# Batch 0 of a convolution and low-rank mixer kernel: U in float32 on a hardware queue, x in pieces of 8, 6 and 3 tiles, and h of group 0 from four partial sums

## The chip, the cores and the metric

The kernel runs on one core of a Trainium2 chip. The metric is the device time of one execution in microseconds (us). A core has a matrix engine (TensorE, "PE", with its weight loads listed apart as "PEld"), VectorE (DVE), ScalarE (ACT), GpSimd (POOL) and SyncE (SP). PE writes its results to PSUM, which has eight banks here; ACT and DVE copy them out to SBUF ("evacuate" them). Data come from the chip's main memory by 16 DMA engines. POOL's loads go through a software queue and can change the type on the way (float32 to bfloat16); loads issued by SP and ACT go through hardware queues.

## The reference

```python
# x: (8, 4224, 192), weight: (8 heads, 7 taps), U: (4224, 32), V: (32, 4224)
w = exp(weight - weight.max(-1, keepdims=True)); w = w / (w.sum(-1, keepdims=True) + 1e-9)
x_pad = concat([zeros((B, 6, D)), x], axis=1)              # causal, along the sequence
y[b, s, h*24 + g] = sum_k w[h, k] * x_pad[b, s + k, h*24 + g]
hT = y.transpose(0, 2, 1) @ U @ V                          # mixes along the sequence
u  = y + hT.transpose(0, 2, 1)
out = u + maximum(u @ w_ch1, 0) @ w_ch2                    # 192 -> 768 -> 192
```

Each head's convolution has 7 taps that are the softmax of its row of `weight`. All inputs and the output are float32; the kernel computes in bfloat16 with float32 sums.

## The kernel before, in words

**Tiles and groups.** The sequence of each of the 8 batches is cut into 33 tiles of 128 positions. `y[b]` holds a batch as 128 positions x 33 tiles x 192 channels. Eight consecutive tiles, counted over all batches, form a group; there are 33 groups. For each group the kernel makes `u`, transposes it to channels on partitions (`uT`), multiplies by W1 with a relu (`w1`, PE line 590, evacuations at lines 601 and 603), multiplies by W2 and adds `u` (`w2`, line 614), and stores (line 629).

**Batch 0, the part before group 0.** This is a chain of its own, in the order in which the code is written (the order of each engine's instructions is the order of the code; nothing is rearranged):

- `w_sb` comes by SP's queue (L61). x of batch 0 lies in SBUF as 64-row blocks, two halves of partitions (`r` = 0 and 1), and is loaded by POOL in two pieces, of 13 and 4 tiles per half (`KP`, L86 to L95, L135; issued at L79).
- POOL makes index patterns with iota (`dif`, `tap`, `fp`, `efp`, L101 to L123). DVE compares them to one-hot patterns, takes the softmax (L192 to L213, the exponential on ACT at L201), and forms `pr` (L223). `band_half` sums `pr` with seven products by the identity (L231) and copies the result to `band`, the banded matrix of a head's taps, by four evacuations on ACT (L240) for each half of the heads.
- POOL loads U as bfloat16 (`Ur`, L130 and L134), V's first 2,048 columns (`V0_sb`, 32 partitions, L139), W1 in four loads (L143), V (L153, L160), W2 (L164), then x of batch 1.
- `idle` runs matrix products of zeros (L173), 60 ahead of the band and 30 ahead of the convolution, each of 128 columns.
- `conv` (L368) makes y by products of `band` with x (L381), with one evacuation by ACT and one by DVE (`evac`, L272 and L274) for each call. Piece 0 has one call for each of the 8 heads, piece 1 two calls of 4 heads.
- `u_layout` (L276) rearranges U by products with `Eq` (L281) into `U_sb`, with tiles' positions on partitions.
- `yT_part(0)` (L542) starts `uT` of group 0 in three banks with products by the identity (L548).
- `tt` is yT U for the batch, 32 ranks x 192 channels. `tt_mm` (L405) lets four tiles work at once, so that it leaves four partial sums in four groups of 32 partitions. For batch 0 the first piece's partial sums go to `tf` (`tt_first`), a product by `R4f` (L701) adds them and repeats the sum on all four groups, and `tt_more` (L451) adds the tiles of the second piece with weights repeated four times (`U4_sb`, L435). `tt_done` copies the result out (L461).
- `hT_part(0)` (L558) adds V0 times tt to the three banks (L563), and ACT and DVE copy them out as `uT`. Then `w1(0)` starts. After it, `hT_part(1)` does the same for group 1.

**Later batches.** `tt_split` copies the partial sums as a bfloat16 value and a bfloat16 remainder (`hi`, `lo`, L425), `tt_sum` adds the four groups by `R4` (L467), and the work is placed between the groups by the hand-written table `SLOTS`. Loads of later batches are held until a named product of `w1` has ended (`held`, `LOADS`), and from batch 2 on POOL makes a shifted copy of x (`x_shift`, L306 to L318) for a convolution in 32-column tiles (`conv32`, L352).

Of the kernel before, what the change touches and what calls it, by code (L numbers as in the profile page):

```python
# [7 lines left out]
ALU = mybir.AluOpType  # L8
# [6 lines left out]
def kernel(  # L15
# [43 lines left out]

    w_sb = cst.tile([P, H, KC], F32, name="w_sb")  # L60
    nc.sync.dma_start(out=w_sb[:], in_=weight[:].partition_broadcast(P))  # L61
    xt = [None] * B
# [23 lines left out]
    KP = [(0, 13), (13, NB1 // 2)]  # L86

    def x_piece(k):
        for r in range(2):
            k0, k1 = KP[k]  # L90
            k1 = min(k1, (NB0, NB1)[r] // 2)
            x_part(0, r, (1 - r if k == 0 else 2 * k0 + 1), 2 * k1 + 1)

    x_tile(0)
    x_piece(0)  # L95
# [5 lines left out]
    dif = cst.tile([P, BW], F32, name="dif")  # L101
    for r in range(4):
        nc.gpsimd.iota(
            dif[QB * r : QB * r + QB, :],
            pattern=[[1, BW]],
            base=0,
            channel_multiplier=-1,
            allow_small_or_imprecise_dtypes=True,
        )
    tap = cst.tile([P, KC], F32, name="tap")  # L110
    nc.gpsimd.iota(
        tap[:],
        pattern=[[-1, KC]],
        base=HW,
        channel_multiplier=0,
        allow_small_or_imprecise_dtypes=True,
    )

    fp = cst.tile([P, P], I32, name="fp")
    nc.gpsimd.iota(fp[:], pattern=[[1, P]], base=P, channel_multiplier=-1)  # L120

    efp = cst.tile([P, 4, P], I32, name="efp")
    nc.gpsimd.iota(efp[:], pattern=[[-1, 4], [1, P]], base=4 * P, channel_multiplier=-4)  # L123


    NUB = (NT + 3) // 4
    Ur = cst.tile([P, NUB, 4 * R], BF16, name="Ur")
    U4 = moe_U[:].rearrange("(n a) r -> n (a r)", a=4)
    nfull = NT // 4
    nc.gpsimd.dma_start(  # L130
        out=Ur[:, 0:nfull, :], in_=U4[0 : nfull * P, :].rearrange("(k p) c -> p k c", p=P)
    )
    nlast = NT * 32 - nfull * P
    nc.gpsimd.dma_start(out=Ur[0:nlast, nfull, :], in_=U4[nfull * P :, :])  # L134
    x_piece(1)  # L135


    V0_sb = cst.tile([32, 2 * GT * P], BF16, name="V0_sb")
    nc.gpsimd.dma_start(out=V0_sb[:], in_=moe_V[:, 0 : 2 * GT * P])  # L139
# [27 lines left out]
    zz = cst.tile([P, 512], BF16, name="zz")  # L167
    nc.vector.memzero(zz[:])  # L168

    def idle(n, w):  # L170
# [6 lines left out]
    idle(60, P)  # L177
# [5 lines left out]
    x_zero(0, nc.vector)  # L183
    hot = cst.tile([P, KC, BW], BF16, name="hot")
# [4 lines left out]
        op=ALU.is_equal,  # L189
    )  # L190
# [10 lines left out]
    nc.scalar.activation(e_sb[:], d_sb[:], ACT.Exp)  # L201
    ident = cst.tile([P, P], BF16, name="ident")
# [18 lines left out]
    def band_half(hh):  # L221
# [16 lines left out]
        for r in range(4):  # L238
            o = QB * (r % 2)
            nc.scalar.activation(  # L240
                out=band[QB * r : QB * r + QB, HQ * hh : HQ * hh + HQ, o : o + BW],
                in_=bp[QB * r : QB * r + QB, 0 : HQ * BW].rearrange("p (h t) -> p h t", h=HQ),
                func=ACT.Copy,
            )

    band_half(0)
    band_half(1)


    Eq = cst.tile([P, 4, P], BF16, name="Eq")  # L250
    nc.vector.tensor_scalar(
        out=efp[:], in0=efp[:], scalar1=P - 1, scalar2=None, op0=ALU.bitwise_and
    )
    nc.vector.tensor_scalar(
        out=Eq[:], in0=efp[:], scalar1=0.0, scalar2=None, op0=ALU.is_equal
    )
    nc.vector.tensor_scalar(
        out=fp[:], in0=fp[:], scalar1=R - 1, scalar2=None, op0=ALU.bitwise_and
    )
    R4f = cst.tile([P, P], F32, name="R4f")  # L260
    nc.vector.tensor_scalar(
        out=R4f[:], in0=fp[:], scalar1=0.0, scalar2=None, op0=ALU.is_equal
    )
    R4 = cst.tile([P, P], BF16, name="R4")
    nc.vector.tensor_copy(out=R4[:], in_=R4f[:])

# [9 lines left out]
    def u_layout():  # L276
# [12 lines left out]
        for jj in range(4):  # L289
            evac(  # L290
                "AD"[jj % 2],
                U_sb[:, 0 : nb[jj], jj, :],
                up[jj][:, 0 : nb[jj] * R].rearrange("p (k r) -> p k r", r=R),
            )

# [72 lines left out]
    def conv(b, h0, nh, rs, engs, k0=0, k1=NT):  # L368
# [4 lines left out]
        pp = {r: bank() for r in rs}  # L373
# [31 lines left out]
    def tt_mm(b, js, p=None, o=0):  # L405
# [3 lines left out]
        for n, j in enumerate(js):  # L409
            c = n % 4  # L410
            nc.tensor.matmul(  # L411
                out=p[32 * c : 32 * c + 32, o : o + D],
                lhsT=U_sb[:, j // 4, j % 4, :],
                rhs=yt[b][:, j, :],
                start=(n < 4),
                stop=(n + 4 >= len(js)),
# [11 lines left out]

    def tt_first(p, js, rest):


        U4_sb = cst.tile([P, sum(b - a for a, b in rest), 4, R], BF16, name="U4_sb")
        n = 0
        for a, b in rest:
            nc.vector.tensor_copy(  # L435
                out=U4_sb[:, n : n + b - a, :, :],
                in_=U_sb[:]
                .rearrange("p k j r -> p (k j) r")[:, a:b, :]
                .unsqueeze(2)
                .to_broadcast([P, b - a, 4, R]),  # L440
            )
            n += b - a
        p = tt_mm(0, js, p, 256)
        t = sml.tile([P, D], F32, name="tt_f", bufs=1)
        evac("A", t[:], p[:, 256 : 256 + D])
        return U4_sb, t

# [241 lines left out]
    for h in range(H):  # L689
        conv(0, h, 1, [0, 1], "AD", *KP[0])  # L690
# [108 lines left out]
```

## Time and profile before

| | us |
|---|---|
| median of 9 runs (lowest to highest) | 330.86 (330.03 to 331.65) |
| the profiled execution's own time | 330.86 |
| its span | 328.9 |
| PE busy | 318.9 (97%) |
| DVE busy | 268.7 (82%) |
| ACT busy | 171.0 (52%) |
| POOL busy | 141.9 (43%) |
| x_sb, first load of batch 0: issue to landing | 7.2 |
| x_sb, second load of batch 0: issue to landing | 10.1 |
| Ur, first load: issue to landing | 8.3 |
| V0 (V_sb, 128 KB): issue to landing | 8.1 |

Times in the profile are counted from the start of the span. A line such as `12.98 2.44 DVE y_sb L274 x6` in the chain of waits is start, length, engine, tile, line of the code and number of instructions; each piece of the chain is what released the next. In the timeline a line is start, length, engine, line, operation, what is written from what, shapes, count, and in brackets how long the engine was idle before and what it waited for. A busy PE is not a PE at its peak, because products overlap. KB of a load are counted as written.

### The profile page before, as it was taken

How to read it: one execution, taken by the hardware profiler on the slowest of the kernel's cores; microseconds unless marked ns; L12 is line 12 of the kernel's file. 1: busy time of each engine (PE TensorE's matmuls, PEld its weight loads, DVE VectorE, ACT ScalarE, POOL GpSimd, SP SyncE). 2: the span in 40 equal slices, each digit the busy share in tenths (PEclk: the TensorE clock that was granted, in tenths of full speed). 3: DMA queues.
4: the chain of work that ended last, by engine and by line, in shares of the span. 5: the costliest groups of instructions: out<-in, count | busy, mean ns of one | idle time of the engine just before them, and what ended most of it. 6: DMA issues, size and time to landing. Idle time of an engine off the chain costs nothing.

```text
span 328.9 us, 9736 instructions
## 1 busy us (share of the span) xinstructions
PE 318.9 (97%) x4072; PEld 224.4 (68%) x4072; DVE 268.7 (82%) x547; ACT 171.0 (52%) x351; POOL 141.9 (43%) x109
## 2 busy tenths in 40 slices
PE   7889999999999999999999999999999999999995
PEld 7655676567647846966874785587797487487495
DVE  5757999996986997798698789879897897896863
ACT  1658444563586098158519807843902912912910
POOL 8580229854995695968659599000000000000000
PEclk9999999999999999999999999999999999999999
DMA  8999996799999899699889969039559159249035
GB/s 102 192 171 165 155 204 153 145 191 158 264 200 171 163 185 199 158 225 200 171 201 169 202 162 216 24 100 240 74 135 261 39 132 216 88 117 268 3 121 169
DMA packets 122908, 53.54 MB, mean 163 GB/s; under 512 B 87760, under 2 KB 122832, under 8 KB 122864
## 3 DMA queue, kind: packets, MB, share of 16 engines
q1 hardware_dynamic: 84672, 38.18, 50.7%
q0 software_dynamic: 38192, 14.73, 38.9%
q8 instruction: 32, 0.52, 0.7%
q14 instruction: 12, 0.10, 0.1%
HBM read 29.49 MB, written 25.95 MB: 169 GB/s over the span
## 4 chain that ended last, share of the span: by engine, by line
PE 78%; POOL 8%; DMA 7%; DVE 3%; ACT 3%; issue 1%; POOLq 0%; DVEq 0%
PE ps L614 37%; PE ps L590 32%; DMA x_sb<-in_x_dram 7%; POOL xb_sb L318 5%; PE ps L352 3%; PE ps L496 3%; ACT rl_sb L601 2%; PE ps L411 2%; DVE y_sb L274 2%; POOL x_sb L79 1%; POOL xb_sb L306 1%; DVE rl_sb L603 1%; PE ps L381 0%; PE ps L467 0%; DVE uT L274 0%
## 5 line engine op out<-in xcount | busy, mean ns | idle before, releaser
L601 ACT ACTIVATE rl_sb<-ps 128x512 bf16<-128x512 f32 x235 | 125.3, 605 | 111.0 <-PE ps L590 99.1
L614 PE MATMUL ps<-W_sb,rl_sb 128*128 128x192 bf16 x1584 | 141.7, 246 | 0.2
L614 PEld LDWEIGHTS <-rl_sb 128*128 128x128 bf16 x1584 | 128.0, 98 | 13.4 <-issue 12.8
L590 PE MATMUL ps<-uT,W_sb 64*128 64x512 bf16 x1188 | 132.0, 376 | 0.8 <-DVE uT L274 0.8
L603 DVE TENSOR_SCALAR rl_sb<-ps 128x512 bf16<-128x512 f32 x161 | 104.3, 689 | 17.7 <-PE ps L590 17.4
L590 PEld LDWEIGHTS <-W_sb 64*128 64x128 bf16 x1188 | 63.9, 94 | 64.6 <-issue 5.0
L622 DVE TENSOR_TENSOR out_sb<-ps,u_sb 128x384 f32<-128x384 f32 (+1 forms) x133 | 70.3, 550 | 24.8 <-PE ps L614 22.4
L318 POOL COPY xb_sb<-x_sb 32x3072 bf16<-32x3072 bf16 (+1 forms) x24 | 67.6, 2824 | 0.7
L518 DVE TENSOR_TENSOR u_sb<-y_sb,ps 128x192 bf16<-128x192 bf16 (+1 forms) x168 | 66.3, 461 | 0.0
L306 POOL COPY xb_sb<-x_sb 128x3072 bf16<-128x3072 bf16 x12 | 32.7, 2742 | 29.7 <-PE ps L352 15.9
L272 ACT ACTIVATE y_sb<-ps 128x384 bf16<-128x384 f32 (+3 forms) x90 | 36.9, 504 | 10.4 <-PE ps L352 7.6
L79 POOL DMA_DIRECT2D x_sb<-in_x_dram x32 | 27.0, 851 | 27.2 <-PE ps L590 16.2
L274 DVE CAST y_sb<-ps 128x408 bf16<-128x408 f32 (+2 forms) x42 | 20.8, 549 | 3.6 <-PE ps L381 2.9
L496 PE MATMUL ps<-tt_sb,V_sb 32*128 32x192 bf16 x264 | 12.6, 246 | 0.8 <-DVE tt_sb L461 0.6
L352 PE MATMUL ps<-xb_sb,band 64*32 64x384 bf16 (+1 forms) x192 | 12.4, 332 | 0.5 <-POOL xb_sb L318 0.5
L352 PE MATMUL ps<-x_sb,band 64*32 64x384 bf16 x192 | 12.1, 333 | 0.0
L496 PEld LDWEIGHTS <-V_sb 32*128 32x128 bf16 x264 | 4.7, 92 | 8.2 <-issue 8.2
L173 PE MATMUL ps<-zz 128*128 128x128 bf16 x90 | 7.9, 271 | 1.2 <-DVE zz L168 1.2
L173 PEld LDWEIGHTS <-zz 128*128 128x128 bf16 x90 | 7.6, 128 | 1.2 <-DVE zz L168 1.2
L352 PEld LDWEIGHTS <-band 64*32 64x32 bf16 x384 | 4.6, 89 | 4.8 <-issue 3.7
L381 PE MATMUL ps<-x_sb,band 64*64 64x312 bf16 (+3 forms) x192 | 7.2, 277 | 0.7 <-DMA x_sb<-in_x_dram 0.7
L425 ACT ACTIVATE tt_hi<-ps 128x192 bf16<-128x192 f32 x7 | 2.3, 331 | 10.8 <-PE ps L411 10.8
(64 smaller groups left out, 71.8 us busy)
## 6 DMA issues: line engine op xcount, KB each, us to landing
out_dram<-out_sb SPq DMA_DIRECT2D x131, 192.0 KB, 2.9
x_sb<-in_x_dram POOLq DMA_DIRECT2D x14, 384.0 KB, 7.3
x_sb<-in_x_dram POOLq DMA_DIRECT2D x7, 432.0 KB, 7.3
x_sb<-in_x_dram POOLq DMA_DIRECT2D x7, 408.0 KB, 6.7
x_sb<-in_x_dram POOLq DMA_DIRECT2D x1, 648.0 KB, 10.1
x_sb<-in_x_dram POOLq DMA_DIRECT2D x1, 624.0 KB, 7.2
uT<-u_sb SPq DMA_TRANSPOSE x31, 4.4
W_sb<-in_moe_w_ch_dram POOLq DMA_DIRECT2D x2, 192.0 KB, 5.3
```

The costliest lines, as they stand in the source:

```text
L79: return nc.gpsimd.dma_start(out=xt[b][HB * r : HB * r + HB, s0:s1, :], in_=x[b, blk * HB : (blk + s1 - s0) * HB, :].rearrange("(j p) d -> ...
L272: nc.scalar.activation(out=out, in_=in_, func=ACT.Copy)
L274: nc.vector.tensor_copy(out=out, in_=in_)
L306: nc.gpsimd.tensor_copy(out=xbt[b][:, s0:s1, :], in_=xt[b][:, s0 + 1 : s1 + 1, :])
L318: nc.gpsimd.tensor_copy(out=xbt[b][q, s0:s1, :], in_=xt[b][q, s0:s1, :])
L352: nc.tensor.matmul(out=pp[r][QB * cg : QB * cg + QB, 0 : nk[r] * GS], lhsT=w[hr], rhs=t[hr, st : st + 2 * nk[r] - 1 : 2, hs], start=True, ...
L518: nc.vector.tensor_tensor(out=u_group(g)[:, i : i + n, :, hf, :], in0=yt[b][:, run[0] : run[0] + n, :].rearrange("p n (c k) -> p n c k", c=3),
L590: last = nc.tensor.matmul(out=pp[hf][:], lhsT=W1_sb[HB * hf : HB * hf + HB, c, m * P : (m + 1) * P], rhs=uTt[g][HB * hf : HB * hf + HB, :, ...
L601: nc.scalar.activation(out=rl[:, m, hf, :], in_=pp[hf][:], func=ACT.Relu)
L603: nc.vector.tensor_scalar_max(out=rl[:, m, hf, :], in0=pp[hf][:], scalar1=0.0)
L614: nc.tensor.matmul(out=cps[:, a * D : (a + 1) * D], lhsT=rlt[g][:, m, hf, (i + a) * P : (i + a + 1) * P], rhs=W2_sb[:, m, :], start=(m == ...
L622: nc.vector.tensor_tensor(out=o[:, 0:n, :].rearrange("p n (c k) -> p n c k", c=3), in0=cps[:, 0 : n * D].rearrange("p (n c k) -> p n c k", ...
```

## The change

- U is loaded as float32 by two loads on ACT's hardware queue, issued ahead of x. ACT copies it to bfloat16 after the exponential. `u_layout` moves ahead of `band_half`; all four of its evacuations are on ACT.
- x of batch 0 comes in pieces of 8, 6 and 3 tiles (2 in the first half). The two halves of a piece are loaded by calls of their own; the first half of piece 0 goes ahead of the iotas, the second half after three of them.
- `dif` is one iota and gets its offsets by a DVE addition of `rq`; `efp` is float32 and is compared with `rq`, so the bit operations on it go. The second half of `band` is evacuated by ACT and DVE in turn.
- `V0_sb` has 128 partitions: V's first 1,024 columns stand on all four groups of 32, by four loads.
- Fillers: 140 of 16 columns and 20 of 128 ahead of `u_layout`, 20 of 64 and 20 of 32 around the second half of `band`.
- Piece 0 of conv takes two heads a call, piece 1 three, three and two, piece 2 four and four; pieces 1 and 2 share two pairs of banks.
- `tt` of batch 0 stays four partial sums in one bank. `tt_split` makes hi and lo of all 128 rows, and `hT_part(0)` multiplies both with the 128-row `V0_sb`, which adds the groups in the product. `tt_first`, `tt_more`, `R4f` and `U4_sb` go. For group 1, `tt_sum(0)` runs after `w1(0)`.

```diff
@@ ahead of x
+    Uf = cst.tile([P, NUB, 4 * R], F32, name="Uf")
+    nc.scalar.dma_start(
+        out=Uf[:, 0:nfull, :], in_=U4[0 : nfull * P, :].rearrange("(k p) c -> p k c", p=P)
+    )
+    nc.scalar.dma_start(out=Uf[0:nlast, nfull, :], in_=U4[nfull * P :, :])
@@ POOL's order
-    KP = [(0, 13), (13, NB1 // 2)]
+    KP = [(0, 8), (8, 14), (14, NB1 // 2)]
-    x_piece(0)
+    x_piece(0, 0)
-    for r in range(4):
-        nc.gpsimd.iota(dif[QB * r : QB * r + QB, :], ...)
+    iota(dif[:], [[1, BW]], 0, -1)
+    iota(tap[:], [[-1, KC]], HW, 0)
+    iota(efp[:], [[-1, 4], [1, P]], 0, -4)
+    x_piece(0, 1)
     nc.gpsimd.iota(fp[:], pattern=[[1, P]], base=P, channel_multiplier=-1)
-    nc.gpsimd.dma_start(out=Ur[:, 0:nfull, :], ...)
-    nc.gpsimd.dma_start(out=Ur[0:nlast, nfull, :], in_=U4[nfull * P :, :])
-    x_piece(1)
-    V0_sb = cst.tile([32, 2 * GT * P], BF16, name="V0_sb")
-    nc.gpsimd.dma_start(out=V0_sb[:], in_=moe_V[:, 0 : 2 * GT * P])
+    for k in (1, 2):
+        for r in range(2):
+            x_piece(k, r)
+    V0_sb = cst.tile([P, 2 * GT * P], BF16, name="V0_sb")
+    for r in range(4):
+        w = (2 if r == 0 else 1) * GT * P
+        nc.gpsimd.dma_start(out=V0_sb[QB * r : QB * r + QB, 0:w], in_=moe_V[:, 0:w])
@@ fillers, patterns, band
+    rq = cst.tile([P, 2], F32, name="rq")
+    for r in range(4):
+        for n, v in enumerate((32.0, -128.0)):
+            nc.vector.memset(rq[QB * r : QB * r + QB, n : n + 1], v * r)
-    idle(60, P)
+    idle(140, 16)
+    idle(20, P)
+    nc.vector.tensor_scalar(
+        out=dif[:], in0=dif[:], scalar1=rq[:, 0:1], scalar2=None, op0=ALU.add
+    )
...
+    nc.vector.tensor_scalar(
+        out=Eq[:], in0=efp[:], scalar1=rq[:, 1:2], scalar2=None, op0=ALU.is_equal
+    )
     nc.scalar.activation(e_sb[:], d_sb[:], ACT.Exp)
+    nc.scalar.activation(out=Ur[:, 0:nfull, :], in_=Uf[:, 0:nfull, :], func=ACT.Copy)
+    nc.scalar.activation(out=Ur[0:nlast, nfull, :], in_=Uf[0:nlast, nfull, :], func=ACT.Copy)
...
-    band_half(0)
-    band_half(1)
+    u_layout()
+    band_half(0, "A")
+    idle(20, 64)
+    band_half(1, "AD")
+    idle(20, 32)
@@ h of a group
     def hT_part(g, tp, engs):
+        ts = ttb[0] if g == 0 else [ttb[0]]
+        k = P if g == 0 else R
+        for n, t in enumerate(ts):
+            for c in range(3):
+                for hf in range(2):
+                    nc.tensor.matmul(
+                        out=tp[c][HB * hf : HB * hf + HB, :],
+                        lhsT=t[0:k, HB * c : HB * c + HB],
+                        rhs=V0_sb[0:k, (2 * g + hf) * 4 * P : (2 * g + hf + 1) * 4 * P],
+                        start=False, stop=(n + 1 == len(ts)), tile_position=(0, HB * hf),
+                    )
@@ the chain before group 0
-    idle(30, P)
-    for h in range(H):
-        conv(0, h, 1, [0, 1], "AD", *KP[0])
-    u_layout()
+    for h in range(0, H, 2):
+        conv(0, h, 2, [0, 1], "AD", *KP[0])
     yT = yT_part(0)
-    U4_sb, tf = tt_first(ps0, ...)
-    for h in range(0, H, 4):
-        conv(0, h, 4, [0, 1], "AD", *KP[1])
-    nc.tensor.matmul(out=ps0[:, 0:D], lhsT=R4f[:], rhs=tf[:], start=True, stop=False)
-    tt_more(ps0, U4_sb, rest)
-    tt_done(0, ps0)
+    ps0 = tt_mm(0, js[0], last=False)
+    work = [{0: bank(), 1: bank()} for _ in range(2)]
+    for n, (h, nh) in enumerate(((0, 3), (3, 3), (6, 2))):
+        conv(0, h, nh, [0, 1], "AD", *KP[1], pp=work[n % 2])
+    for n, h in enumerate(range(0, H, 4)):
+        conv(0, h, 4, [0, 1], "AD", *KP[2], pp=work[1 - n % 2])
+    tt_mm(0, js[1], ps0, first=False, last=False)
+    tt_mm(0, js[2], ps0, first=False)
+    tt_split(0, ps0)
     hT_part(0, yT, "AD")
@@ after w1(0)
+                tt_sum(0)
                 hT_part(1, yT_part(1), "AD")
```

## The prediction

> **What bounds the kernel now.** I read the chain of waits first, cut to the first 45 us, since every edit but one lies ahead of the first matmul of group 0 (L590). Columns: start, length, what.
>
> ```profile
> 1.26 1.12 POOL x_sb L79
> 2.38 10.07 DMA x_sb<-in_x_dram
> ...
> 12.49 0.47 PE ps L381 x6
> 12.95 0.02 issue
> 12.98 2.44 DVE y_sb L274 x6
> ...
> 19.77 0.37 DVE tt_sb L461
> 20.14 0.04 issue
> 20.18 0.42 PE ps L563 x2
> ...
> 21.52 1.08 PE ps L590 x6
> 22.61 4.50 ACT rl_sb L601 x9
> 27.11 0.29 ACT uT L272
> ```
>
> The first 12.45 us are the landing of the second half of piece 0; then 9.03 us of work, mostly evacuations, bring the first L590 at 21.52. After that ACT paces group 0. Later the chain is mostly PE; where it passes to POOL, POOL's load at 61.62 waited 1.39 us for an L590 matmul. So time won ahead of 21.52 should reach the end nearly whole.
>
> Next the stretches of 1 us (busy time of PE, PEld, DVE, ACT, POOL, then clock, DMA share, GB/s), and the timeline of POOL and ACT:
>
> ```profile
> 2.00:3.00 1.00, 1.00 (x13) 1.00 (x11) 0.00 (x0) 0.03 (x1) 1.00 (x2) 1.00 0.09 22
> 3.00:4.00 1.00, 1.00 (x12) 1.00 (x11) 0.00 (x0) 0.00 (x0) 0.82 (x4) 1.00 0.75 61
> 4.00:5.00 1.00, 1.00 (x12) 1.00 (x10) 0.39 (x2) 0.00 (x0) 0.88 (x5) 1.00 1.29 146
> 5.00:6.00 1.00, 1.00 (x13) 1.00 (x11) 0.75 (x6) 0.25 (x1) 1.00 (x2) 1.00 1.60 190
> ```
> ```profile
> 8.69 2.44 ACT L240 ACTIVATE band<-ps 32x152 bf16<-32x152 f32 x8 [2.99 <-PE ps L231]
> ...
> 12.73 0.63 POOL L143 DMA_DIRECT2D W_sb<-in_moe_w_ch_dram  x1 [2.93 <-DMA x_sb<-in_x_dram]
> ...
> 18.57 3.38 POOL L79 DMA_DIRECT2D x_sb<-in_x_dram  x4
> ```
>
> The DMA engines fill only from 5 us on; until about 19 us they then hold some 190 GB/s. `band` was ready at 11.13, so x came last. The tenth POOL load, a piece of W1, waited for the second to land: the trace looks like eight loads open at a time.
>
> **U ahead of x.** Two POOL issues (0.92 and 0.53 us) go; two issues on ACT's queue come, each like w_sb's on SP (0.40), ahead of a table load of 1.28, with ACT idle until 5.45. U is 540 kB read either way. An x packet writes 384 B for 768 B read, and 495 of them in the full us at 5 read 380 kB; U is thus 1.4 us of the engines. Between 2 and 5 us they moved 341 kB less than 3 x 190, that is 1.8 us lie free. So U costs x between 0 and 1.4 us; I take 0.7, as its landing reaches into the full time.
>
> When does U land? The hardware queue's nearest rows are w_sb (128 packets, 2.9 us) and a store of out (256 packets, 2.0 us from issue to landing in the quiet stretch 319.7 to 321.4). w_sb, issued at 0.75, had 7 packets out before 2.0, so some 1.1 us pass first; a store then has 0.9 for 256, 3.5 ns each. U has 1,024 and 32: 0.75 + 1.1 + 3.5, I take **5.3**. The high end is w_sb's pace, 107 packets in the us from 2 to 3, near 10 ns: 10.3 us, a landing at 12. The low end, twice the stores' pace, is 3.7. The wait for U is new: ACT's copies stand before it, and behind them on ACT the evacuations of U_sb and of both halves of band, for which all of conv waits.
>
> The Trainium skill, "DMA: Bandwidth & Descriptors", section "Issuing engines are not separate DMA queues", speaks against this edit: loads of all queues share the same 16 engines, so another queue saves issue time only. By the rule alone x pays the full 1.4 us and conv starts 0.7 later than my sum; the trace's free 1.8 us is why I charge half.
>
> **Piece 0 of 8 tiles.** 384 + 408 KB are 811 kB against 1,303. By the 1-us rows 811 kB of x have gone by 8.2 us and 1,303 by 10.8; the old piece landed at 12.45, 1.65 behind the mean, which I scale to 1.0. Landing: 8.2 + 1.0 + 0.7 = **9.9** (9.2 to 10.6). Pieces 1 and 2 (576 and 240 KB, 3.1 and 1.3 us) land near 14.0 and 15.5; old piece 1, behind the same U and x, landed at 15.99.
>
> **The band.** dif's iota was four (0.84), now one (0.2), but fp's now stands behind the issue of x's second half (0.9) and DVE's ident waits for it, with the softmax queued behind. POOL: 1.26 + 0.84 issue, iotas to 3.2, issue to 4.1, fp to 4.35. w_sb lands at 3.65; eight memsets on DVE (0.1 each) end before. pr begins at 5.5 (6.71 before), both halves done at 8.0. But u_layout now stands ahead of band_half on PE and ACT: U 5.3, the copies to bf16 on ACT (1,024 columns; 256 took 379 ns and 512 605, so 1.06, and 0.27): 6.65; 16 matmuls 0.99, four ACT evacuations at 0.31: 8.9; the first half's four at 0.31: 10.1; the second, half on DVE, 10.6. Conv can start at **10.3**, where band and x meet: 2.2 ahead of 12.49. U late by one us makes this late by one.
>
> **Fillers.** The first 60, of 128 columns, start 107 ns apart up to 6.2 us (row below) and 56 later, where a row lasts 219 ns; the clock column reads 1.00 throughout, so I go by the durations. Fillers of 16 columns have no row. Bounds: 13 ns apart (L496, 8 in 0.34 us at 246 each) and 107. I take 28, the pitch of L548 (24 in 0.86 at 221), whose weights are the narrowest beside a full set of rows: 3.9 us from 1.2, then 20 wide ones, ending at 7.0, when U's copy is ready: nothing on the path. At 56 they end near 10.5 and conv slips by 3.5. The two later sets of 20 lie under ACT's evacuations.
>
> ```profile
> L173 PE MATMUL ps<-zz x12: 314/314/314, 3.0 to 4.2; 128*128 128x128 bf16 x12
> ```
>
> The Trainium skill, "TensorE: Matmul & The Clock Gate", Part 1, says about 3.4 us of sustained activity lifts the clock; the step from 314 to 219 ns agrees. No run here shows whether 16 columns count as activity; by the page's floor of 25 ns for a narrow matmul the set is an estimated 3.5 us.
>
> **Conv to the first L590.** Piece 0: four calls, DVE evacuations of 384 columns at 0.48 (L274: 548 ns, 475 apart): 10.3 + 0.5 + 1.9 = 12.75 (8 x 0.39 before). yT 0.86: 13.6. Sixteen tt matmuls 0.5: 14.1. Piece 1, landing about 14.0: three calls, 0.5 to the first result, evacuations 0.52, 0.52, 0.4: 16.4. Piece 2: its matmuls from 16.0, two evacuations at 0.4: 17.3. Last tt matmuls 0.3: 17.6. R4f's products (0.59), the seven of L451 (0.81) and the copies to tt_f and U4 are gone. tt_split: ACT 0.33 gives hi at 18.0; DVE's lo (0.36) hides under hi's six products. Those are six more at 512 columns in pairs, 0.64; then as before 1.34 to L590: **20.0**, 1.5 ahead of 21.52. V0 in four loads (0.56 issue each on POOL, 393 kB more read, 1.0 us of the engines) must land by 18.0; behind 4.2 us of piece 1 and 2 and its own 1.7 it lands near 17.3. That wait is close: past 18.0 each us costs one. W1 follows by 19.0. Batch 1's loads leave POOL some 1.2 later than 18.57 and band2's copies behind them; batch 1's packets had run dry by 31 and its conv began at 40.99, which covers it.
>
> **tt_sum(0).** Two more matmuls and a DVE cast (0.36) before group 1's products, the cast behind DVE's last relu (to 26.55). yT_part(1) covers PE, not the cast: +0.4 (0 to 0.7).
>
> **Sum.** 1.5 - 0.4 = 1.1; I take 1.0, as 0.1 of piece 1's wait seems likely. Span 328.9 - 1.0 = 327.9; with the 1.96 us around it 329.9. The profiled execution's own time, 330.86, is the median of the runs shown.
>
> **Rivals.**
> (1) *U becomes the late load: slower.* For: w_sb's 10 ns per packet, and both hardware queues start at 0.75. Against: stores run at 3.5 ns. The gain is gone when U lands at 6.4; at 5 ns per packet it lands at 7.1, with x sharing the engines about 8, conv starts at 13.0, and 330.86 + 1.6 = 332.5; at 10 ns, 336.5. Chance 0.20.
> (2) *Fillers run long or leave PE slow: slower or level.* PE work of some 4 us from 7 to 18 would take the 314 ns form; half of it is on the path: +2.0, net 331.9. Against: the 20 wide ones. Chance 0.12.
> (3) *The bytes decide.* All of x and V0 must come anyway; if piece 2 lands at 16.0 and V0 at 18.5, L590 starts at 20.5: gain 0.6, 330.3. For: 190 GB/s without a gap. Chance 0.20.
> (4) More than forecast: U wholly in the free time and tt_sum covered, 329.2. Chance 0.08.
> Forecast as worked out: 0.40.
>
> **Numbers.** 0.2%, 0.66 us, is about what a measurement of this kernel can tell. Faster: 0.36 of the forecast, 0.08, and 0.08 of (3): 0.52. Slower: 0.18 of (1) and 0.09 of (2), 0.02 of the rest: 0.29. Same: 0.19. The range goes from 328.9, (4) and a little, to 332.8, past (1)'s middle and (2); (1) at w_sb's pace is left out. The forecast's own range is 329.2 to 330.6.
>
> **What would show it.** Right: U landed by 5.5, first y_sb evacuation near 10.8, first L590 near 20.0, group 1's L590 near 26.8 (27.90). Wrong: u_layout's L281 waiting for U or for L173; L563 waiting for V_sb; x's second half landing past 11; y evacuations waiting for piece 2 past 16.5. The prediction falls if the first L590 is not ahead of 21.0, or if it is and the end is not.

## The result and the profile after

The changed kernel takes **336.1 us** (median of 10 runs, 334.01 to 337.56) beside 330.8 us of the kernel before on the same chip: **1.0157 of it, 95% interval 1.0134 to 1.018**. It is slower by 5.3 us (5.2 by the ratio), outside the range forecast and on the other side. The profiled execution has a span of 334.2 us, 5.3 more than before.

The chain of waits of the kernel after, cut to the first 39 us (line 572 makes the first products of a group, which was line 590; 596 was 614; line 389 is `conv`, 272 `u_layout`, 243 `band_half`, 173 the fillers, 544 `hT_part`, 419 `tt_mm`):

```profile
0.75 7.18 DMA Uf<-in_moe_U_dram
7.95 1.06 ACT Ur L212
...
9.26 1.11 PE ps L272 x11
10.37 1.00 PE ps L243 x7
11.37 1.07 PE ps L173 x20
12.44 0.89 PE ps L243 x7
13.32 0.50 PE ps L173 x20
13.82 0.86 PE ps L389 x34
...
17.94 0.45 issue
...
21.72 1.22 issue
22.94 0.26 PE ps L419
23.22 0.34 ACT tt_hi L433
23.56 0.04 issue
23.60 1.94 PE ps L544 x8
25.56 0.39 ACT uT L263
25.98 0.44 DVE uT L265
26.41 0.04 issue
26.45 0.82 PE ps L572 x4
...
33.33 1.08 PE ps L572 x6
...
37.99 1.15 PE ps L596 x12
```

The two lines of the kernel before for the last two:

```profile
27.90 1.08 PE ps L590 x6
...
32.55 1.15 PE ps L614 x12
```

The head of the chain is no longer x but U. `conv` starts at 13.82 on the chain, where 12.49 was. Then there are two pieces that the chain of before doesn't have at all: "issue" of 0.45 and 1.22, in which PE waits for nothing that the profile shows. The products of `hT_part` take 1.94 on the chain instead of 0.42. The first product of group 0 comes at 26.45 instead of 21.52, **4.93 late**, and later the first L596 (L614 before) at 37.99 instead of 32.55, 5.44 late. So what was lost ahead of group 0 reaches the end whole, with 0.5 more between the first products of groups 0 and 1 (6.88 against 6.38).

The timeline of the kernel after (start, length, engine, line, operation; in brackets the idle time before and what ended it):

```profile
5.51 0.21 DVE L201 TENSOR_REDUCE mx_sb<-w_sb 128x8 f32<-128x56 f32 x1 [1.27 <-DMA w_sb<-in_weight_dram]
7.95 1.06 ACT L212 ACTIVATE Ur<-Uf 128x1024 bf16<-128x1024 f32 x1 [1.70 <-DMA Uf<-in_moe_U_dram]
...
10.30 1.07 PE L243 MATMUL ps<-pr,ident 128*128 128x152 bf16 x7
...
12.99 0.49 POOL L134 DMA_DIRECT2D V_sb<-in_moe_V_dram  x1 [1.32 <-DMA x_sb<-in_x_dram]
...
13.68 0.31 DVE L265 CAST band<-ps 32x152 bf16<-32x152 f32 x1 [3.97 <-ACT band L263]
...
14.33 1.75 ACT L263 ACTIVATE y_sb<-ps 128x384 bf16<-128x384 f32 x4
15.21 1.95 DVE L265 CAST y_sb<-ps 128x384 bf16<-128x384 f32 x4
...
18.39 0.69 PE L389 MATMUL ps<-x_sb,band 64*64 64x144 bf16 x32 [0.45 <-issue]
...
22.94 0.24 PE L419 MATMUL ps<-y_sb,U_sb 128*32 128x192 bf16 x1 [1.22 <-issue]
23.60 1.49 PE L544 MATMUL ps<-V_sb,tt_hi 128*64 128x512 bf16 x6 [0.42 <-ACT tt_hi L433]
```

Both loads on the hardware queues are late (w_sb held DVE for 1.27, U held ACT for 1.70), and POOL's load at 12.99 waited for the second half of piece 0, which landed at 12.7, though piece 0 has 38% fewer bytes than before. In the second half of `band`, each evacuation waits for the one before it on the other engine, by semaphores that the program sets; DVE's first evacuation of y starts 0.88 after ACT's. The two PE lines with "issue" stand inside, and ahead of the last product of, a run of like products whose data are there: x's last piece had landed at 17.1, and the last evacuation of y ended at 21.24.

**PE ran slowly up to 13.25.** The seven products of the first half of `band` take 1.07. In the kernel before they took 0.62:

```profile
8.03 0.62 PE L231 MATMUL ps<-pr,ident 128*128 128x152 bf16 x7 [0.78 <-DVE pr L223]
```

They start 126 ns apart, and 65 there. The clock column reads 1.00 for both, but a stretch for which the trace holds no record of the clock counts as 1.00 in it, and the first record stands at 13.25 in the kernel after and at 6.54 in the kernel before. Like products change their pace at the first record: the fillers of the kernel before go from 107 to 56 ns at 6.5, and with U behind piece 0 (below), where the first record is at 9.50, the products of the second half of `band` go from 331 to 229 ns in length at 9.5. So ahead of the first record the column is not to be believed, and PE went at half its pace.

Stretches of the kernel after (busy time of PE, PEld, DVE, ACT, POOL, then granted clock, DMA share, GB/s):

```profile
5.00:6.00 1.00, 1.00 (x13) 1.00 (x11) 0.46 (x3) 0.00 (x0) 1.00 (x3) 1.00 1.30 177
6.00:7.00 1.00, 1.00 (x10) 0.80 (x9) 0.72 (x5) 0.25 (x1) 1.00 (x2) 1.00 1.34 154
```
```profile
22.00:24.00 2.00, 0.64 (x3) 0.18 (x4) 0.36 (x1) 0.33 (x1) 2.00 (x4) 0.87 0.88 74
24.00:26.00 2.00, 2.00 (x12) 0.72 (x8) 0.02 (x1) 0.40 (x2) 1.89 (x4) 0.50 1.56 186
26.00:28.00 2.00, 1.89 (x14) 0.68 (x14) 1.25 (x3) 1.04 (x3) 1.26 (x4) 0.77 1.58 194
```

While U's packets and x's share the engines, these move 177 and 154 GB/s written where x alone moved 190 and 183 in the kernel before. That the sharing lowers the rate is not shown: with U ahead of x in the kernel before (below) the two moved 204 and 193, and with U behind piece 0, where nothing but x and one code packet came in these 2 us, 168 and 127. And after the second stop of PE the granted clock falls to a half, just when `hT_part`'s twelve wide products come.

**Where the 4.93 us are.** `conv` starts 1.33 later. (With the fillers of before, in the first run below, U lands as late, at 7.9, and `conv` starts at 12.24. So late U uses up what the smaller piece 0 was to win, and the 1.33 on top are from the fillers and the slow PE.) PE's instruction stream stands still from 17.72 to 18.39 and from 21.46 to 22.94, start to start, 2.15 in all (the idle time in the brackets is less, 1.67, as the products ahead of the stops have modelled ends that run on). Without these stops the way from `conv` to `tt_split` is 23.22 - 13.82 - 2.15 = 7.25, against 12.49 to 19.77 = 7.28 before: level. From there to the first product of group 0 it is 3.23 against 1.75, 1.48 more, of which the slow clock is 0.86 (below) and the remainders of hi and lo 0.64. Sum: 1.33 + 2.15 - 0.03 + 1.48 = 4.93.

**What the stops are.** They end at PE's 706th and 962nd instruction, counted from the start with weight loads, products and the few instructions on semaphores, so 705 and 961 stand ahead of them; between lie 256. The queue named "instruction" moved these packets in the kernel after, in the view of queues (packets, MB, share of 16 engines):

```profile
q8 instruction: 33, 0.54, 0.7%
```

That is 16 KB each, or 64 bytes for each of 256 instructions. The Trainium skill, "Runtime: NRT & Kernel Launch", section "Instruction fetch mechanics", says that an engine's code comes in blocks of 256 instructions of 16 KiB by the sequencer's own DMA, and that the cost of crossing into a block is mostly hidden. The number and the size agree with the queue's line; "mostly hidden" is what the runs below test.

### The profile page after: what moved, and what is told of

The parts are those of the page before. It is cut to its first block, busy times and chain, and to the rows that moved or that the text cites. A ratio compares the mean times of both kernels' runs of the same rounds, so it can differ in the third digit from the quotient of the medians.

```text
span 334.2 us, 10110 instructions
## 1 busy us (share of the span) xinstructions
PE 322.4 (96%) x4252; PEld 226.1 (68%) x4252; DVE 269.0 (80%) x552; ACT 172.7 (52%) x352; POOL 142.7 (43%) x109
## 4 chain that ended last, share of the span: by engine, by line
PE 90%; DVE 4%; DMA 2%; ACT 2%; issue 1%
PE ps L596 40%; PE ps L572 38%; PE ps L359 3%; PE ps L474 3%; DMA Uf<-in_moe_U_dram 2%; PE ps L419 2%; DVE y_sb L265 1%; DVE rl_sb L585 1%; PE ps L389 1%; ACT rl_sb L583 1%; PE ps L544 1%; DVE u_sb L496 1%; PE ps L243 1%; PE ps L173 0%; PE ps L445 0%
## 5 line engine op out<-in xcount | busy, mean ns | idle before, releaser
L596 PE MATMUL ps<-W_sb,rl_sb 128*128 128x192 bf16 x1584 | 141.7, 246 | 0.1
L596 PEld LDWEIGHTS <-rl_sb 128*128 128x128 bf16 x1584 | 128.0, 98 | 13.4 <-issue 12.8
L263 ACT ACTIVATE y_sb<-ps 128x408 bf16<-128x408 f32 (+4 forms) x89 | 37.2, 505 | 10.9 <-PE ps L359 6.8
L89 POOL DMA_DIRECT2D x_sb<-in_x_dram x34 | 28.2, 837 | 30.5 <-PE ps L572 19.1
L265 DVE CAST y_sb<-ps 128x408 bf16<-128x408 f32 (+3 forms) x41 | 21.0, 559 | 1.8 <-PE ps L389 1.6
L359 PE MATMUL ps<-xb_sb,band 64*32 64x384 bf16 x192 | 12.1, 332 | 0.0
L419 PE MATMUL ps<-y_sb,U_sb 128*32 128x192 bf16 x264 | 8.2, 248 | 1.7 <-issue 1.2
L173 PE MATMUL ps<-zz 128*128 128x16 bf16 (+3 forms) x200 | 8.0, 195 | 1.0 <-DVE zz L163 1.0
L389 PE MATMUL ps<-x_sb,band 64*64 64x192 bf16 (+5 forms) x256 | 7.8, 249 | 0.7 <-issue 0.5
## 6 DMA issues: line engine op xcount, KB each, us to landing
x_sb<-in_x_dram POOLq DMA_DIRECT2D x2, 288.0 KB, 10.3
```

Source lines behind the costliest of these rows:

```text
L89: return nc.gpsimd.dma_start(out=xt[b][HB * r : HB * r + HB, s0:s1, :], in_=x[b, blk * HB : (blk + s1 - s0) * HB, :].rearrange("(j p) d -> ...
L263: nc.scalar.activation(out=out, in_=in_, func=ACT.Copy)
L359: nc.tensor.matmul(out=pp[r][QB * cg : QB * cg + QB, 0 : nk[r] * GS], lhsT=w[hr], rhs=t[hr, st : st + 2 * nk[r] - 1 : 2, hs], start=True, ...
L596: nc.tensor.matmul(out=cps[:, a * D : (a + 1) * D], lhsT=rlt[g][:, m, hf, (i + a) * P : (i + a + 1) * P], rhs=W2_sb[:, m, :], start=(m == ...
```

## The experiments

Four theories stood. *U*: its load ahead of x delays x, and its landing holds ACT and PE. *Code*: PE waits for its own instructions, because pieces and fillers raise their number ahead of group 0 from 630 to 989. *Fillers*: the narrow ones don't bring PE to full pace. *h*: the new way to h costs more than it saves. Ratios are to the kernel before, with their 95% intervals.

**The fillers of before, in the kernel after.**

```diff
-    idle(140, 16)
-    idle(20, P)
+    idle(60, P)
...
-    idle(20, 64)
...
-    idle(20, 32)
```

> The changed kernel with the fillers of before (60 of 128 columns at the start, none around band): 280 PE instructions fewer ahead of group 0. Theory 'code': the two waits of PE at 17.72 and 21.46, which stand exactly 256 PE instructions apart and end after a 16 KB instruction packet, are waits for code; both go, the clock stays up for L544 (0.43 to 0.22 a pair), and the first L572 comes near 23.2 instead of 26.45: about 333. Theory 'x': the waits are for x pieces 1 and 2; they stay, and the time stays near 336.

Measured: 333.65 us, 1.0083 (1.0052 to 1.0114). `conv` starts at 12.24 and PE is fast (first clock record at 4.34, the products of `band` 66 ns apart): the fillers are worth some of it. But a stop is there again, at another place. Timeline:

```profile
18.20 0.75 PE L386 MATMUL ps<-x_sb,band 64*64 64x144 bf16 x35 [1.17 <-issue]
```

It comes ahead of PE's 450th instruction, 256 before the 706th. With 280 instructions less for a start, the block ends 13 products further on in `conv` of piece 1 (29 of its products stand ahead of the stop, 16 in the kernel after), and the stop is there. Piece 1 of x had landed at 14.91, so the stop is no wait for x. The expectation that the stops would go did not come true; it named the right cause.

**U behind piece 0, as bfloat16 by POOL's queue, with `u_layout` behind the first conv; the fillers of after.**

```diff
-    nc.scalar.dma_start(out=Uf[:, 0:nfull, :], ...)
-    nc.scalar.dma_start(out=Uf[0:nlast, nfull, :], ...)
...
+    nc.gpsimd.dma_start(out=Ur[:, 0:nfull, :], ...)
+    nc.gpsimd.dma_start(out=Ur[0:nlast, nfull, :], ...)
     for k in (1, 2):
...
-    nc.scalar.activation(out=Ur[:, 0:nfull, :], in_=Uf[:, 0:nfull, :], func=ACT.Copy)
-    nc.scalar.activation(out=Ur[0:nlast, nfull, :], in_=Uf[0:nlast, nfull, :], func=ACT.Copy)
...
-    u_layout()
     band_half(0, "A")
...
+    u_layout()
     yT = yT_part(0)
```

> The changed kernel with U as in before: by POOL in bfloat16 behind piece 0, no copies on ACT, u_layout between conv of piece 0 and yT; fillers as in the changed kernel. Theory 'U': U ahead of x holds both x (second half of piece 0 landing near 12.9) and the band; piece 0 now lands near 10, the first conv evacuation near 11, and 2.5 to 3.5 us come back ahead of tt unless the waits for code eat them: 333 to 334. Theory 'code alone': conv starts no earlier than 13, the time stays at 336.

Measured: 331.57 us, 1.0018 (0.9991 to 1.0046): no difference from before that can be told. `conv` starts at 10.36. This one edit takes back 1.4% of the 1.6%. Stops remain, but short: 0.40 ahead of the 706th and 0.67 ahead of the 962nd, of which only some 0.2 can count, as PE there waits for `tt_hi` up to 19.58 in any case. The first product of group 0 is at 21.83, not ahead of 21.52, though `conv` is 2.1 ahead: x's last piece landed at 15.86 (15.71 before), since x has the same bytes however it is cut.

**U by the hardware queue alone, in the kernel before** (two ACT loads ahead of x, the copies on ACT; `u_layout` where it was).

```diff
+    nc.scalar.dma_start(out=Uf[:, 0:nfull, :], ...)
+    nc.scalar.dma_start(out=Uf[0:nlast, nfull, :], ...)
     xt = [None] * B
...
-    nc.gpsimd.dma_start(out=Ur[:, 0:nfull, :], ...)
-    nc.gpsimd.dma_start(out=Ur[0:nlast, nfull, :], ...)
...
     nc.scalar.activation(e_sb[:], d_sb[:], ACT.Exp)
+    nc.scalar.activation(out=Ur[:, 0:nfull, :], in_=Uf[:, 0:nfull, :], func=ACT.Copy)
+    nc.scalar.activation(out=Ur[0:nlast, nfull, :], in_=Uf[0:nlast, nfull, :], func=ACT.Copy)
```

> The kernel before with the U part alone: U in float32 by ACT's queue ahead of x, two copies on ACT behind the exponential, u_layout where it was. Theory 'U': x, which waits 0.8 us longer for its first packets and shares the engines until 7.5, lands some 1.0 later than 12.49, and w_sb near 5.5; band near 13; 331.5 to 332.5. If U fills idle time only: 330.5 to 331.

Measured: 332.31 us, 1.0063 (1.0035 to 1.0091). The chain of waits:

```profile
2.38 12.46 DMA x_sb<-in_x_dram
...
23.92 1.08 PE ps L593 x6
```

x's first piece landed at 14.85, 2.4 later than before (2.38 + 10.07), and the first product of group 0 is 2.4 later. ACT's copies of U end at 8.6, ahead of `band`'s first evacuation, so U itself holds nothing here: the loss is x's delay alone. The U theory stands, with a price of its own, 1.6 us by the medians (2.1 by the ratio), without any of the other edits.

The Trainium skill, "DMA: Bandwidth & Descriptors", section "Issuing engines are not separate DMA queues", says that loads from all engines run on the same 16 DMA engines and interleave. Read so, x pays for U's bytes in full, which the prediction worked out as 1.4 us and charged at half. In this run x landed 2.4 later: the rule holds, and 1.4 is too low a price. By 7.0 us POOL's queue had moved 0.24 MB, where it had moved 0.58 in the kernel before; that alone is 1.8 us at 190 GB/s.

**The fillers of after, in the kernel before.**

```diff
-    idle(60, P)
+    idle(140, 16)
+    idle(20, P)
...
-    idle(30, P)
+    idle(20, 64)
+    idle(20, 32)
```

> The kernel before with the fillers of the changed kernel (140 of 16 columns and 20 of 128 at the start, 20 of 64 and 20 of 32 ahead of conv): 220 PE instructions more. Theory 'code': the boundary that lay in w1(0) now lies some 4.4 us behind the one ahead of it, against 4.6 to 5 needed for a packet of code, so one wait of 0.3 to 0.6 ahead of group 0, and slow products at the band: 331.3 to 332. If fillers cost nothing: 330.8.

Measured: 332.23 us, 1.0043 (1.0017 to 1.0069). No stop for code stands out. Piece 0's end landed at 13.12 (12.45 before), and the first conv took 3.95 of PE time on the chain where evacuations had paced it (12.49 to about 15.4): the products ran slow, and the first clock record is at 16.55. From 24 to 26 the clock is 0.50. The fillers theory holds, at 1.5 us (332.23 less 330.72), and what the narrow fillers fail to do is raise the clock. In the three kernels with 140 of 16 columns the first record is at 9.50, 13.25 and 16.55; in the fourteen other traces, with fewer narrow ones or none, at 4.2 to 6.9. Why products of 16 columns do not raise it is not shown.

**Both undone together** (fillers of before, U behind).

```diff
-    idle(140, 16)
-    idle(20, P)
+    idle(60, P)
...
-    u_layout()
     band_half(0, "A")
...
+    u_layout()
     yT = yT_part(0)
```

> The changed kernel with both undone: U by POOL in bfloat16 behind piece 0 with u_layout behind conv of piece 0, and the fillers of before (60 of 128 columns). If U and the code waits are the whole loss, this is level with the kernel before or ahead of it: first L568 near 21.2 (21.83 with the many fillers), 330.3 to 331.3. If three pieces and two-part h cost more than they save, it stays above 331.5.

Measured: 333.46 us, 1.0069 (1.0046 to 1.0093). The two gains do not add; it is slower than U behind alone. In this run PE is idle for most of 5.97 to 10.84, and the clock is 0.66 from 12 to 16. x also landed later than with U behind alone (second half of piece 0 at 10.80 instead of 9.62, piece 1 at 14.94 and 16.46 instead of 12.64 and 14.16), with the same bytes in the same order; why is not known.

**The same, with the second half of `band` all on ACT and the making of R4 behind `tt_split`**, so that DVE is free for y ("third candidate"); and that **with two pieces, 8 and 9 tiles** ("second candidate").

```diff
-    band_half(1, "AD")
+    band_half(1, "A")
...
     tt_split(0, ps0)
+    nc.vector.tensor_scalar(out=fp[:], ...)
+    nc.vector.tensor_scalar(out=R4[:], ...)
```
```diff
-    KP = [(0, 8), (8, 14), (14, NB1 // 2)]
+    KP = [(0, 8), (8, NB1 // 2)]
```

> As after_both, and DVE kept free for y: the second half of band evacuated by ACT alone and the two operations for R4 behind tt_split. In after_u_behind DVE began its first y evacuation at 11.83, 0.9 after ACT, behind two band casts that waited in turn with ACT's and the R4 operations. If that delay is on the path, the first L568 comes 0.5 to 0.9 earlier than in after_both: 329.5 to 330.5. If the code waits pace conv, no change.

> As cand3 with two pieces, of 8 and 9 tiles, instead of three: 128 PE instructions and 64 products fewer, piece 1 in four calls of two heads. Theory 'code': fewer instructions, no wait at the 449th or 705th; conv of piece 1 then waits for the landing of all of x near 15.5 to 16. If x decides: 0.3 to 0.5 later than cand3; if code decides: 0.3 to 0.8 earlier.

Measured: 332.17 us, 1.0033 (1.0011 to 1.0055), and 332.69, 1.0046 (1.0024 to 1.0067). DVE's first y is at 10.59, as the prediction had it (10.8). Neither is ahead of before. (The profiled executions are 1.2 and 1.4 us quicker than these medians, so the traces do not show all that the others lose.) In the third candidate the stop is at the 450th instruction again. Timeline:

```profile
16.25 2.65 PE L375 MATMUL ps<-x_sb,band 64*64 64x144 bf16 x99 [1.15 <-issue]
```

After it the clock is 0.57 from 16 to 20. The second candidate has no such stop; PE waits for piece 1 until 16.08, and the clock falls likewise. So a low clock follows a wait for data as well as a wait for code.

**The way to h alone, in the kernel before**: `tt_split`, the 128-row products, V0 by four loads, `tt_sum(0)`; measured twice.

```diff
-    U4_sb, tf = tt_first(ps0, ...)
+    ps0 = tt_mm(0, js[0], last=False)
...
-    nc.tensor.matmul(out=ps0[:, 0:D], lhsT=R4f[:], rhs=tf[:], start=True, stop=False)
-    tt_more(ps0, U4_sb, rest)
-    tt_done(0, ps0)
+    tt_mm(0, js[1], ps0, first=False)
+    tt_split(0, ps0)
...
+                tt_sum(0)
                 hT_part(1, yT_part(1), "AD")
```

> The kernel before with the h part alone: four partial sums kept, tt_split, 128-row products with V0 in four loads, tt_sum(0) behind w1(0). It saves R4f's products, the seven of L451 and the U4 copies (some 1.3 us) and costs 0.3 of split, 0.64 of products and 0.4 of tt_sum: 330.5 to 331.0. If V0's four loads come late behind x, L563 waits for them: 331.5 to 332.5.

> before_h once more, with more rounds: 0.9986 of the kernel before in the first series (0.9966 to 1.0006). If the h part gains, 0.9975 to 0.9995 and the interval below 1; if it is level, 0.9995 to 1.0010.

Measured: 330.72 us, 0.9986 (0.9966 to 1.0006), and 330.99, 0.9992 (0.9971 to 1.0013). Level: the h theory falls, and so would a gain from h. `hT_part` starts at 19.82 (20.18 before) but has twelve products, and the first product of group 0 is at 21.81.

**Fewer and wider fillers**: 512 columns instead of narrow ones, in four kernels: after (14, 3 and 2 of them), the third and second candidates (14 and 6), and the way to h alone (14 and 8).

```diff
-    zz = cst.tile([P, P], BF16, name="zz")
+    zz = cst.tile([P, 512], BF16, name="zz")
...
-    idle(140, 16)
-    idle(20, P)
+    idle(14, 512)
```

> The changed kernel with fillers of 512 columns in place of the narrow ones: 14 at the start, 3 and 2 around the second half of band, for about the same time on PE (6 us) with 362 PE instructions fewer. U stays ahead of x. Theory 'code': no wait at the 705th or 961st instruction, and the clock holds; first L572 near 23 instead of 26.45, 332.8 to 333.5. If the fillers' instructions do not matter and only their time does: 335.5 to 336.5.

> cand3 (U by POOL behind piece 0, DVE kept free, three pieces, 128-row h) with fillers of 512 columns: 14 at the start, 6 ahead of conv. cand3 lost 1.37 us at its 449th PE instruction and then ran with the clock at 0.57. Theory 'code and clock': both go, the first product of group 0 comes near 20.8 (22.22 in cand3, 21.52 before) and the time is 330.0 to 330.5. If the landing of x decides (piece 2 near 16.2), 330.8 to 331.5.

> cand2 (two pieces, of 8 and 9 tiles) with the wide fillers. By 'code and clock' the wait is gone as in cand3_wide; piece 1 is whole only near 16.0, so the first product of group 0 comes 0.3 to 0.6 behind cand3_wide: 330.3 to 331.2.

> before_h (the kernel before with the h part alone) with fillers of 512 columns, 14 at the start and 8 ahead of conv, in place of 90 of 128. 136 PE instructions fewer in a kernel that shows no wait for code: within 0.2% of before_h, which was 0.9986 of the kernel before (0.9966 to 1.0006); the spread over executions may shrink if some of them do wait for code.

Measured, in that order: 334.22 us, 1.009 (1.0062 to 1.0118); 331.77, 1.001 (0.9983 to 1.0037); 332.2, 1.0028 (0.9997 to 1.006); 332.41, 1.0031 (1.0006 to 1.0057). The first fell between its two forecasts, with a stop of 1.07 at the 450th instruction that was not expected and a clock at half from 20.0 to 26.9. The third candidate lost its stop of 1.37 (0.25 is left) and its slow clock, and the first product of group 0 came at 21.00; its time lies above both of its forecasts, and that of the second candidate above its own (clock at half from 17.1 to 23.9). The last was expected to have no stop, for it has 22 fillers where the way to h alone had 90 and no stop. Its timeline has one:

```profile
17.17 0.79 PE L383 MATMUL ps<-x_sb,band 64*64 64x72 bf16 x57
18.84 0.28 PE L383 MATMUL ps<-x_sb,band 64*64 64x72 bf16 x7 [0.88 <-issue]
```

It comes ahead of the 450th instruction, 256 ahead of the 706th. So it isn't the number of instructions by itself. Fewer fillers moved the start of that block from the fillers (194th instruction at 10.84) into conv (14.35), and PE ran through it in 3.41 us instead of 6.19.

**The blocks placed by count**: the number of fillers in the kernel after (85 of 16 columns and 30 of 128, then 3 and 2 of 512) and in the third candidate (38 and 50, then 1 and 5), chosen so that blocks end where PE waits anyway. U stays ahead of x in the first.

```diff
-    idle(140, 16)
-    idle(20, P)
+    idle(85, 16)
+    idle(30, P)
...
-    idle(20, 64)
+    idle(3, 512)
...
-    idle(20, 32)
+    idle(2, 512)
```

> The changed kernel with 85 fillers of 16 columns and 30 of 128 at the start and 3 and 2 of 512 around the second half of band: 230 filler instructions ahead of u_layout. By count the 193rd PE instruction then passes near 4 us, the 449th in yT_part near 15 and the 705th in conv of piece 2 near 20, each more than 4.6 us behind the one ahead. If the count decides, the waits are at most 0.3 each, and what is left is U ahead of x: conv from 13.6, the first L572-like product near 23.5, 332.6 to 333.4. If waits for code come wherever PE is fast, they stay and the time is 334 or more.

> cand3 (U by POOL behind piece 0, DVE kept free) with 38 fillers of 16 columns and 50 of 128 at the start and 1 and 5 of 512 around the second half of band. The 193rd instruction passes near 8 us, the 449th in the tt products near 13.5, the 705th at the end of conv of piece 2 near 18. If the count decides: no wait over 0.3, the first product of group 0 near 20.8, 330.0 to 330.6. If it still waits at the 449th: 331.5 or more.

Measured: 332.59 us, 1.0045 (1.0026 to 1.0064), and 332.84, 1.0049 (1.0025 to 1.0074). The first came out at the lower edge of what was expected if the count decides. Timeline of after, placed by count:

```profile
19.53 0.45 PE L389 MATMUL ps<-x_sb,band 64*64 64x48 bf16 x32 [0.16 <-issue]
...
21.25 0.84 PE L544 MATMUL ps<-V_sb,tt_hi 128*64 128x512 bf16 x6 [0.43 <-ACT tt_hi L433]
```

The stop at the 706th has shrunk from 0.67 to 0.35, the other lies behind group 0's start, and `hT_part` runs at full clock (six products 0.84 long, 1.49 before; to the first product of group 0 1.99 instead of 2.85, 0.86 less). Group 0 starts at 23.24 instead of 26.45, with U as late as ever (landed at 7.71). Of these 3.21 us, 1.80 are the shorter stops (2.15 less 0.35), 0.86 the clock in `hT_part`, and 0.53 an earlier `conv` (13.29), for the edit changed the fillers' work as well: with the 30 wide ones the first clock record is at 5.55, and the clock was at half again only from 8.96 to 12.38. So of the **3.5 us** that lie between the two kernels (336.1 - 332.6; by the two ratios 1.57 - 0.45 = 1.12%, 3.7 us), some 2.7 are code waits with the clock that falls after them. What is left over the kernel before, 1.5, is close to the 1.6 that U ahead of x cost by itself, but the stop that remains, the two-part h and `tt_sum(0)` are in it too. The shares of the causes overlap: U behind takes back 4.5 us, the fillers of before 2.5, and together they are more than the loss. The second was a miss: a stop of 1.17 ahead of the 706th instruction, U landed only at 13.1 in the profiled run, and no gain.

**The stops side by side**, from the traces; "packet" is the last 16 KB packet of the instruction queue ahead of the stop:

| kernel | ahead of instruction | PE stands still | packet | packet to resumption |
|---|---|---|---|---|
| after | 706 | 17.72 to 18.39 | 16.01 | 2.38 |
| after | 962 | 21.46 to 22.94 | 20.67 | 2.27 |
| after, fillers of before | 450 | 16.81 to 18.19 | 16.01 | 2.18 |
| after, U behind | 706 | 15.48 to 15.88 | 13.61 | 2.27 |
| after, U behind | 962 | 18.95 to 19.62 | 17.40 | 2.22 |
| third candidate | 450 | 14.88 to 16.25 | 13.76 | 2.49 |
| after, wide fillers | 450 | 19.04 to 20.11 | 17.76 | 2.35 |
| way to h, wide fillers | 450 | 17.76 to 18.84 | 16.45 | 2.39 |
| after, by count | 706 | 19.18 to 19.53 | 17.26 | 2.27 |
| third candidate, by count | 706 | 18.11 to 19.28 | 16.98 | 2.30 |

All ten resume 2.2 to 2.5 us after a packet starts, at counts that differ by multiples of 256. In the kernel before, the packet came at 13.34 and PE reached its 450th instruction at 17.09, 3.7 later: no stop. In none of the seventeen traces does PE pass its 450th, 706th or 962nd instruction less than 2.18 us after the packet of that block. In the ten rows the packets start 1.5 to 3.8 us after PE has begun the block ahead, so a block of 256 instructions takes PE some 4 to 6 us at least. In before, 256 of them took 6.25 (10.84 to 17.09); in after, conv with pieces of 8, 6 and 3 tiles ran through one in 4.25 and through the next in 3.07, and all ten blocks that ended in a stop had been run through in 2.8 to 5.0. The page's "mostly hidden" does not hold for such stretches.

## Why the prediction was wrong, step by step

- **"Conv can start at 10.3"** failed, by U. The step that failed is "I take 5.3" for U's landing, with the pace of stores taken for a load, and "I take 0.7" for what U costs x. (1,056 packets of 3.5 ns are 3.7 us, not the 3.5 added, so the sum gives 5.5; that slip is small.) U landed at 7.9, the first half of x's piece 0 at 10.9 and its end at 12.7 (9.9 forecast); conv started at 13.8. The rival "U becomes the late load" had the place right (U at 8, conv at 13.0, 332.5 us) and a chance of 0.20. It asked for a pace of 5 ns per packet, and the landing at 7.9 is nearer that. That its other price, 336.5 at 10 ns, lies by the measured 336.1 is luck, for U did not land at 12. With U behind x, conv started at 10.36: the working for piece 0 was right, though the late clock stretched `band_half` there too.
- **"The hardware queue's nearest rows"**: w_sb's own row moved. It landed 4.7 us after issue instead of 2.9, because it now shared the queues' start with U. It hid behind U.
- **Fillers, "28 ns"**: 27 ns measured, and their end at 7.0 as forecast. But the rival on a slow PE, with a chance of 0.12, was right too: `band_half`'s products ran 126 ns apart where before had 65, up to 13.25. "The clock column reads 1.00 throughout" misled: the trace of before has no record ahead of 6.54, and the step from 314 to 219 ns is there, 5.3 us after the first filler. The price in the kernel before was 1.5 us, fillers alone.
- **Conv to `tt_split`, "10.3" to "18.0"**, 7.7: measured 7.6 to the end of `tt_hi` without the stops (23.55 - 13.82 - 2.15). The evacuations were sized well. The landings of pieces 1 and 2 held nothing up here, as conv was late itself; with U behind they came at 14.16 and 15.86 (14.0 and 15.5 forecast). There group 0 began at 21.83 and not at 20.0: `u_layout` stood behind piece 0 again, and a stop took 0.40; the rest was not taken apart. "Old piece 1 landed at 15.99" is the time of POOL's next load; the landing was at 15.71.
- **"h of group 0"**: twelve products at full clock and `tt_split` cost what was said; measured alone, level. V0 was not late in any run: its last load landed 1.1 to 4.8 us ahead of the end of `tt_hi`, also where the profile names a load of V as the releaser.
- **tt_sum, "+0.4"**: 33.33 - 26.45 = 6.88 between the first products of groups 0 and 1, against 27.90 - 21.52 = 6.38: +0.5. It is 6.69, +0.3, where the clock is full (fillers of before in after, U behind, third candidate, after by count); the other 0.2 is the half clock, which lasts to 26.90.
- **"The end nearly whole"**: right, with the other sign.
- **What no step had**: PE waiting for code, 2.15 us, and the clock that falls in it, 0.86 more ahead of group 0 and 0.2 after. The count of PE's instructions was in the diff to be worked out (110 fillers and 68 products more, each with a weight load), and the profile of before showed the instruction queue's packets; the sum has no term for either. With most of the stops gone, and U as late, the time was 332.6; with them it was 336.1.

The best of the other versions are level with before: the way to h alone (0.9986 and 0.9992) and the third candidate with wide fillers (1.001, its interval on both sides of 1). None is shown to beat it. In that candidate the chain goes from x's last landing, 16.65, to group 0 at 21.00; as x's bytes are fixed, I take it that little can be had here by cutting x into pieces; no run shows a bound.

**Open.** Why the engines move only 127 GB/s from 6 to 7 us even with U behind piece 0, and why x's landing lags so far behind the mean. What sets the 1.5 to 3.8 us before a code packet starts. Why 16-column products do not raise the clock. And the clock falls in some kernels without a stop (0.50 from 24 to 26 with the fillers of after in before); what sets it off there is not settled.

## What to carry to other kernels

Count PE's instructions in every stretch that is meant to go fast: code comes in blocks of 256 by packets of its own, and here a PE that ran through a block in less than some 5 us could stop at the end of it; fillers and smaller pieces are paid for in code, and their number decides where the block ends fall. Whether fillers bring PE to full pace is read from how far apart like products start, since a clock column can read 1.00 where nothing was recorded. A load put ahead of another on an idle-looking queue should be charged to the other in full, and more, until a run shows less; put it behind what is needed first. Undo the parts of a bundle one by one *and* together, since here two repairs that each gained gained less when joined.

## What the runs showed of the hardware that was not expected

- PE stopped 0.35 to 1.48 us at instruction counts 256 apart, in eight kernels, each time resuming 2.2 to 2.5 us after the start of a 16 KB packet on the instruction queue.
- A float32 load of 512 KB by ACT's hardware queue took 7.2 us from issue to landing with x beside it (6.5 in the kernel before with that edit alone), and a 28 KB load on SP's queue beside it took 4.7 (4.4) instead of 2.9.
- The granted clock fell to 0.50 after PE had stood nearly idle for some 2 us (21.5 to 23.5, with one product in them). The Trainium skill, "TensorE: Matmul & The Clock Gate", Part 1, gives an idle window of about 3.4 us for this; here less was enough, and the measurement decides.
- 140 products of 16 columns kept PE busy at 27 ns each and did not raise the granted clock: its first record came at 9.50 to 16.55 in the three kernels with them, at 4.2 to 6.9 in the others, and up to it like products ran at half pace (126 ns apart, where 65 were seen).
